# One-token gated decode on one core: the last half row of wo in 125 and 3 partitions, and three engine programs set to a block boundary

## The chip, the cores and the metric

The kernel runs on one core of one Trainium2 chip. The metric is the device time of one execution in microseconds (us), the median of several runs; lower is better.

## What is computed

One token passes through an attention block with a cached context and through a gated feed-forward block, and a sigmoid gate mixes the two results:

```python
g = sigmoid((x * gate_w).sum())                       # x: 512 values
q = x @ wq                                            # wq: 512 x 4096, 32 heads of 128
p = softmax((q . k_cache) * 128 ** -0.5)              # 8 kv heads x 32768 x 128, 4 query heads on each
a = (p . v_cache).reshape(4096) @ wo                  # v_cache like k_cache; wo: 4096 x 512
b = (silu(x @ w1) * (x @ w3)) @ w2                    # w1, w3: 512 x 1792; w2: 1792 x 512
out = g * a + (1 - g) * b                             # 512 values, all float32
```

Every weight and every cache entry is used once, so the work is mostly the transfer of the two caches (134 MB each) and the weights into the core's memory (SBUF).

## The kernel before, in words

Three SBUF regions, `ra`, `rb` and `rc`, hold 128 partitions x 16384 floats (64 KiB per partition, 8 MiB in all) each. Every large transfer is issued by SyncE (SP), in program order, on one hardware queue. A transfer with 128 partitions of contiguous rows moves one row into each partition.

The order of SP's transfers is written out by hand. First come wq into `rc` and w1, w3 into `rb` (line 36), issued ahead of a barrier of all engines (line 40), then the first half of head 0's keys into `ra` (L133). The loop of lines 138 to 148 issues, for each key/value head, two halves of keys (`ra`, `rb`) and two halves of values (`rc`), each behind a wait that says the region is free again: `c_k` counts the score products that PE has finished, `c_v` the value products. The last head's value halves go into `ra` and `rb` (L151, L153). Then come wo into `rc` as two halves of 128 x 8192 (L157, semaphores `l_wo[0]` and `l_wo[1]`), and, behind a wait on `c_v`, w2 into `ra` in five pieces (L163: 7, 4 and 2 of the 14 blocks of 512 columns; L166: the last block in two halves of 256 columns).

VectorE (DVE) turns the keys block by block (L368) in a hardware loop over the heads and does the maxima and the normalisation. TensorE (PE) runs a hardware loop over the heads as well: score products (L298), value products of the head before (L312), small transposes (L322). ScalarE (ACT) copies scores out of PSUM (L406), takes the exponentials (L412) and copies each head's output (L409); its program is unrolled over the eight heads. GpSimd (POOL) lays out the query windows, four copies for each head (L285), also unrolled.

The end of the kernel is PE's: with the heads' outputs in `oq`, 32 products of `oq` with the 32 blocks of 512 columns of wo (L444, the first 16 behind `l_wo[0]`, the others behind `l_wo[1]`), seven with w2's first piece (L451), and then w2's remaining blocks in quarters of 128 columns (L423), each piece behind its own semaphore. Two copies by DVE and ACT (L485) gather the result, ACT sends it out (L489), and SP waits for that transfer.

```python
wod = wo.rearrange("(p k) e -> p (k e)", k=32)
sp.wait_ge(c_v.sem, 2 * HKV - 2)
for i in range(2):
    sp.dma_start(rc[:, i * half:(i + 1) * half], wod[:, i * half:(i + 1) * half]).then_inc(l_wo[i], 16)
```

The functions that the change touches follow, with the profile's line numbers.

## Time and profile before

| what | value |
|---|---|
| median of 3 runs | 691.75 us (691.72 to 691.81) |
| the profiled execution's own time | 691.74 us |
| span of that execution, first to last instruction | 690.4 us |
| PE busy, share of the span | 349.7 us, 51% |
| DVE busy | 306.9 us, 44% |
| ACT busy | 41.6 us, 6% |
| POOL busy | 7.0 us, 1% |
| read from HBM | 296.23 MB, 429 GB/s over the span |

Busy times say how long an engine had an instruction in work. The core has 16 DMA engines; the shares given for them are means over the 16. The queue q1 carries SP's transfers, q10 ACT's; q8 and q14 carry instructions, which the engines' sequencers fetch in blocks while the program runs. A DMA view of a stretch books a packet by the time at which it starts.

### The profile page before, as it was taken

The numbers are of one execution on the slowest core, as the hardware profiler recorded it, in microseconds if no ns is written. First come the engines' busy times: TensorE is split into PE (matmuls) and PEld (weight loads), VectorE is DVE, ScalarE is ACT, GpSimd is POOL, SyncE is SP. The second block draws the span as 40 slices with busy tenths as digits, with TensorE's granted clock in tenths as the row PEclk, the third lists the DMA queues.
The fourth block names the chain that finished last, engine by engine and source line by source line (L and its number), as shares of the span: only waits on it lengthen the run. The fifth ranks groups of instructions, "written<-read, shape, count | busy, mean of one in ns | idle before, by whom it ended". The sixth has DMA issues, their size and how long they took to land. (4 is left out here: it accounts for less than half of the span.)

```text
span 690.4 us, 6719 instructions
## 1 busy us (share of the span) xinstructions
PE 349.7 (51%) x2946; PEld 112.6 (16%) x2946; DVE 306.9 (44%) x194; ACT 41.6 (6%) x111; POOL 7.0 (1%) x41
## 2 busy tenths in 40 slices
PE   1721645757065721757066721766075712766567
PEld 1200103103011120203021220203021210203122
DVE  1015862991725447091825447091815446191000
ACT  0110011002000010002000010002000010002000
POOL 0000000000000000000000000000000000000000
PEclk9985675988578965889567965988578965878679
DMA  9999999999999999999999999999999999999997
GB/s 414 393 469 426 425 426 427 444 448 429 426 425 440 425 437 452 429 429 425 437 429 429 456 433 429 425 433 433 425 444 444 430 429 425 437 429 429 452 411 320
DMA packets 6079, 296.36 MB, mean 429 GB/s; under 512 B 691, under 2 KB 947, under 8 KB 1078
## 3 DMA queue, kind: packets, MB, share of 16 engines
q1 hardware_dynamic: 6048, 296.23, 99.3%
q8 instruction: 6, 0.10, 0.1%
q14 instruction: 3, 0.02, 0.0%
q10 hardware_dynamic: 22, 0.01, 0.0%
HBM read 296.23 MB, written 0.00 MB: 429 GB/s over the span
## 5 line engine op out<-in xcount | busy, mean ns | idle before, releaser
L368 DVE STREAM_TRANSPOSE rb<-rb 128x2048 f32<-128x2048 f32 x64 | 141.8, 2275 | 130.7 <-DVEq L127 130.7
L312 PE MATMUL psum<-rc,prob 128*32 128x512 f32 x896 | 114.9, 671 | 140.5 <-PEq L127 140.5
L368 DVE STREAM_TRANSPOSE ra<-ra 128x2048 f32<-128x2048 f32 x64 | 141.3, 2274 | 58.3 <-DVEq L127 58.3
L298 PE MATMUL psum<-rb,winbuf 128*32 128x512 f32 x512 | 88.8, 771 | 84.9 <-PEq L127 84.9
L298 PE MATMUL psum<-ra,winbuf 128*32 128x512 f32 x512 | 60.9, 614 | 26.7 <-PEq L127 21.2
L312 PEld LDWEIGHTS psum<-rc,prob 128*32 128x32 f32 x896 | 34.2, 122 | 216.0 <-issue 216.0
L392 DVE TENSOR_REDUCE mx<-psum 128x4 f32<-128x1024 f32 x8 | 9.8, 1225 | 86.9 <-DVEq L127 86.9
L298 PEld LDWEIGHTS psum<-rb,winbuf 128*32 128x32 f32 x512 | 13.0, 120 | 159.1 <-issue 159.1
L406 ACT COPY sbuf<-psum 128x512 f32<-128x512 f32 x16 | 9.9, 616 | 471.1 <-PE psum L298 471.1
L298 PEld LDWEIGHTS psum<-ra,winbuf 128*32 128x32 f32 x512 | 16.8, 112 | 69.4 <-issue 69.4
L412 ACT ACTIVATE prob<-psum,nm 128x256 f32<-128x256 f32 x32 | 18.8, 693 | 47.0 <-DVE nm L400 47.0
L322 PE MATMUL psum<-ident,sbuf 128*64 128x64 f32 x512 | 18.1, 234 | 5.0 <-PEq L127 5.0
L322 PEld LDWEIGHTS psum<-ident,sbuf 128*64 128x64 f32 x512 | 17.0, 148 | 12.5 <-issue 12.5
L373 DVE SCALAR_TENSOR_TENSOR otall<-psum,gate,recip 128x4 f32 (+1 forms) x8 | 1.7, 214 | 33.3 <-DVEq L127 33.3
L345 PE MATMUL psum<-sums,ones 128*128 128x4 f32 x16 | 4.5, 350 | 22.8 <-PEq L127 22.8
L312 PE MATMUL psum<-rb,prob 128*32 128x512 f32 x64 | 8.8, 714 | 9.4 <-DMA rb<-in_A_v_cache_dram 9.4
L312 PE MATMUL psum<-ra,prob 128*32 128x512 f32 x64 | 9.9, 790 | 3.5 <-DMA ra<-in_A_v_cache_dram 3.5
L285 POOL COPY winbuf<-winraw 32x16 f32<-32x16 f32 x32 | 6.1, 190 | 535.7 <-PE psum L298 501.5
L444 PE MATMUL psum<-rc,oq 128*32 128x512 f32 x64 | 9.0, 712 | 3.9 <-DMA rc<-in_A_wo_dram 3.5
L229 PE MATMUL psum<-rc,xp 128*32 128x512 f32 x64 | 8.4, 687 | 4.7 <-DMA rc<-in_A_wq_dram 4.7
L256 PE MATMUL psum<-rb,xp 128*32 128x448 f32 x64 | 7.8, 637 | 5.4 <-DMA rb<-in_B_w_dram 5.3
L214 PE MATMUL psum<-ones,ob 1*128 1x1 f32 x8 | 2.0, 370 | 15.1 <-DMA prob<-in_gate_w_dram 15.1
(62 smaller groups left out, 86.4 us busy)
## 6 DMA issues: line engine op xcount, KB each, us to landing
rc<-in_A_wo_dram SPq DMA_DIRECT2D x2, 4096.0 KB, 45.8
rb<-in_B_w_dram SPq DMA_DIRECT2D x2, 3584.0 KB, 34.1
ra<-in_B_w_dram SPq DMA_DIRECT2D x1, 1792.0 KB, 33.0
ra<-in_B_w_dram SPq DMA_DIRECT2D x1, 1024.0 KB, 35.2
ra<-in_B_w_dram SPq DMA_DIRECT2D x1, 512.0 KB, 35.9
ra<-in_B_w_dram SPq DMA_DIRECT2D x2, 128.0 KB, 35.7
rc<-in_A_v_cache_dram SPq DMA_DIRECT2D x14, 31.1
ra<-in_A_k_cache_dram SPq DMA_DIRECT2D x8, 41.5
```

Source lines behind the costliest of these rows:

```text
L229: m = pe.matmul(pq[b][32 * j:32 * j + 32, :], xp[:, c, :], rc[:, o:o + REP * DH], start=(c == 0), stop=(c == NC - 1),)
L256: i = pe.matmul(ps[32 * j:32 * j + 32, 0:FJ], xp[:, c, :], rb[:, o:o + FJ], start=(c == 0), stop=(c == NC - 1))
L285: pool.tensor_copy(winbuf[32 * r:32 * r + 32, 16:144].rearrange("p (c k) -> p c k", k=32)[:, :, 4 * r:4 * r + REP], winraw[32 * r:32 * r + ...
L298: i = pe.matmul(s_ps[m][32 * g:32 * g + 32, :], winbuf[:, w:w + 32], region.rearrange("p (n c i) -> p c n i", c=4, i=32)[:, c, n:n + 16], ...
L312: i = pe.matmul(o_ps[32 * t:32 * t + 32, :], prob[:, w:w + 32], region[:, n * DH:(n + 4) * DH], start=(r == 0 and g == 0 and f == 0), stop ...
L322: i = pe.matmul(pf[64 * s:64 * s + 64, 64 * a:64 * a + 64], sbuf[:, a].rearrange("p i m -> p (i m)"), ident.rearrange("p (gf r s q) -> p s ...
L345: pe.matmul(mc[:, 0:REP], ones, sums, start=True, stop=True).then_inc(t_n, 1)
L368: dve.transpose(part[:, c], part[:, c]).then_inc(t_tr, 1)
L392: dve.tensor_reduce(mx, pf.rearrange("p (a q) -> p q a", q=REP), axis=AX.X, op=ALU.max).then_inc(t_mx, 1)
L406: act.copy(sbuf[:, :, :, m], s_ps[m].rearrange("p (n i) -> p n i", i=32)).then_inc(t_ev, 1)
L412: act.activation(prob[:, 0:1024].rearrange("p (a n q) -> p n a q", a=16, q=REP)[:, :, :, q], pf.rearrange("p (n a q) -> p n a q", n=16, q= ...
L444: pe.matmul(acc[32 * t:32 * t + 32, :], oq[:, k:k + 32], rc[:, k * D:(k + 1) * D], start=(k < 4), stop=False, skip_group_check=True,)
```

## The change

The diff has two parts.

In the first, an alignment directive is put on the programs of ACT, DVE and POOL, ahead of wq's load and of the barrier. It names 128 slots: where the loader places the program, the instruction that follows stands at a multiple of 128 instruction slots, and the slots skipped are branched over (`max_nops=0`). PE's and SP's programs get none.

In the second, the transfer of wo's second half loses its last 256 columns (half of the last block of 512), so that it moves 128 x 7936 instead of 128 x 8192. Those 256 columns come in two further transfers on the same queue behind it, of partitions 0 to 124 and of partitions 125 to 127. Both count on a new semaphore, `l_wx`, and PE waits for it ahead of the last of the 32 products with wo (k = 31).

```diff
+SHARE = 125
...
     nc = tc.nc
+    for engine in (nc.scalar, nc.vector, nc.gpsimd):
+        engine.addr_align(128, offset=0, max_nops=0)
     rb, rc = (nc.alloc_sbuf_tensor(n, [P, 16384], F32).ap() for n in ("rb", "rc"))
...
+    l_wx = token("l_wx")
...
     for i in range(2):
-        sp.dma_start(rc[:, i * half:(i + 1) * half], wod[:, i * half:(i + 1) * half]).then_inc(l_wo[i], 16)
+        e = slice(i * half, (i + 1) * half - i * D // 2)
+        sp.dma_start(rc[:, e], wod[:, e]).then_inc(l_wo[i], 16)
+    for p in (slice(0, SHARE), slice(SHARE, P)):
+        sp.dma_start(rc[p, W - D // 2:W], wod[p, W - D // 2:W]).then_inc(l_wx, 16)
...
             if k % 16 == 0:
                 pe.wait_ge(l_wo[k // 16], 16)
+            if k == 31:
+                pe.wait_ge(l_wx, 32)
```

SP's program from the last value half to the end, before (line, operation, region and source, partitions x elements):

```order
L153 DMA rb<-in_A_v_cache_dram 128x16384
L157 DMA rc<-in_A_wo_dram 128x8192 x2
L163 DMA ra<-in_B_w_dram 128x3584
L163 DMA ra<-in_B_w_dram 128x2048
L163 DMA ra<-in_B_w_dram 128x1024
L166 DMA ra<-in_B_w_dram 128x256 x2
```

and with the change, whose lines from 161 to 173 are those of wo and w2:

```order
L157 DMA rb<-in_A_v_cache_dram 128x16384
L162 DMA rc<-in_A_wo_dram 128x8192
L162 DMA rc<-in_A_wo_dram 128x7936
L164 DMA rc<-in_A_wo_dram 125x256
L164 DMA rc<-in_A_wo_dram 3x256
L170 DMA ra<-in_B_w_dram 128x3584
L170 DMA ra<-in_B_w_dram 128x2048
L170 DMA ra<-in_B_w_dram 128x1024
L173 DMA ra<-in_B_w_dram 128x256 x2
```

Two transfers more stand between wo's second half and w2; nothing else of SP moved.

The beginning of ACT's program, before:

```order
L519 UNCONDITIONAL_BRANCH
L40 UNCONDITIONAL_BRANCH
L169 DMA ob<-in_A_x_dram 1x512
L170 DMA prob<-in_gate_w_dram 1x8x64
L176 DMA out_dram<-sbuf 1x512
```

and with the change, where the directive is the row of line 32:

```order
L528 UNCONDITIONAL_BRANCH
L32 ISA
L43 UNCONDITIONAL_BRANCH
L176 DMA ob<-in_A_x_dram 1x512
L177 DMA prob<-in_gate_w_dram 1x8x64
L183 DMA out_dram<-sbuf 1x512
```

DVE and POOL get the same row at the same place.

## Rows read from the trace of the kernel before

**Rows 1.** The page: span, DMA busy tenths in 40 slices, queues (packets, MB, share).
```profile
span 690.4 us, 6719 instructions
...
DMA  9999999999999999999999999999999999999997
...
q1 hardware_dynamic: 6048, 296.23, 99.3%
q8 instruction: 6, 0.10, 0.1%
q14 instruction: 3, 0.02, 0.0%
q10 hardware_dynamic: 22, 0.01, 0.0%
```

**Rows 2.** Chain that ended last, in order of time: start us, us, what.
```profile
672.50 3.64 PE psum L444 x32
676.14 3.49 another core or an unknown queue
...
679.67 5.34 PE psum L444 x32
685.01 1.71 PE psum L451 x14
686.72 1.91 PE psum L423 x59
```

**Rows 3.** Line L157, the transfers of wo: ns min/median/max, issue times, then landing.
```profile
L157 SPq DMA_DIRECT2D rc<-in_A_wo_dram x2: 327/380/433, 628.8 to 629.1; - x2
...
DMA to landing us min/median/max: 41.2/45.8/50.5
```

**Rows 4.** Line L166, the last two transfers of w2.
```profile
L166 SPq DMA_DIRECT2D ra<-in_B_w_dram x2: 432/432/432, 652.2 to 652.7; - x2
...
DMA to landing us min/median/max: 35.6/35.7/35.8
```

**Rows 5.** Windows of the end: engines' busy us (x), PEclk, DMA share, GB/s.
```profile
680.00:685.00 5.00, 5.00 (x36) 1.39 (x32) 0.00 (x0) 0.00 (x0) 0.00 (x0) 0.66 0.98 411
...
686.60:687.00 0.40, 0.40 (x22) 0.40 (x23) 0.00 (x0) 0.22 (x1) 0.00 (x0) 1.00 0.45 172
687.00:687.30 0.30, 0.30 (x20) 0.30 (x13) 0.00 (x0) 0.30 (x1) 0.00 (x0) 1.00 0.35 123
687.30:687.60 0.30, 0.30 (x16) 0.16 (x12) 0.00 (x0) 0.06 (x1) 0.00 (x0) 1.00 0.34 120
687.60:688.00 0.40, 0.40 (x18) 0.31 (x20) 0.00 (x0) 0.00 (x0) 0.00 (x0) 1.00 0.13 44
```

**Rows 6.** DMA view by queue, stretch 60 to 680 us.
```profile
q8 instruction: 5, 0.08, 0.0%
```

**Rows 7.** DMA view, stretch 101 to 104 us (one of those five).
```profile
q8 instruction: 1, 0.02, 1.9%
```

**Rows 8.** DMA view, stretch 174 to 176 us.
```profile
q14 instruction: 1, 0.01, 1.0%
```

**Rows 9.** DMA view, stretch 545 to 551 us.
```profile
q14 instruction: 1, 0.01, 0.3%
```

**Rows 10.** DMA view, stretch 638 to 641 us.
```profile
q14 instruction: 1, 0.01, 0.7%
```

**Rows 11.** Timelines of ACT, POOL and DVE: what each ended shortly ahead of a q14 packet.
```profile
172.10 0.22 ACT L412 ACTIVATION_READ_ACCUMULATOR prob<-psum,nm 128x1 f32 x1
...
544.68 0.94 POOL L285 COPY winbuf<-winraw 32x16 f32<-32x16 f32 x4 [77.23 <-PE psum L298]
...
637.59 0.18 DVE L379 RECIPROCAL recip<-psum 128x4 f32<-128x4 f32 x1 [3.25 <-DVEq L127]
```

**Rows 12.** Timeline of the beginning: PE's first large products.
```profile
22.74 8.43 PE L229 MATMUL psum<-rc,xp 128*32 128x512 f32 x64 [4.70 <-DMA rc<-in_A_wq_dram]
```

**Rows 13.** DMA view, stretch 687 to 689 us (packets of 1 KiB, most of them).
```profile
q1 hardware_dynamic: 97, 0.09, 12.9%
```

## The prediction

> **What bounds the kernel now.** Read the page first. The DMA engines are busy at nine tenths or more in every slice but the last, and q1, SP's queue, takes 99.3% of their time for 296.23 MB, while no other engine is busy for much more than half the span [rows 1]. So the kernel lasts as long as its bytes need, and only three things can be saved: the start, the end, and unevenness between the 16 DMA engines. From these rows a packet's price follows: 0.993 x 16 x 690.4 us / 296.23 MB is 37.0 ns for 1000 bytes, 0.303 us for 8 KiB on one DMA engine.

> Second, the chain that ended last: it ends in PE's work on wo and w2, and holds a wait of 3.49 us from 676.14 us [rows 2]. Its end fits the landing of wo's second half: issued at 629.1 us, landed 50.5 us later, at 679.6 us; PE goes on at 679.67 us [rows 2, 3]. The very last link is also a landing: w2's last piece, issued at 652.7 us, lands 35.6 us later, at 688.3 us [rows 4], and the span ends 2.1 us after it. In between PE follows the landings closely.

> Third, the windows of the end, where the reader is to see how the DMA engines run dry: their share is 0.45, then 0.35 and 0.34, then 0.13 [rows 5]. Times 16 that is 7.2 engines busy on average from 686.6 to 687.0 us and 5.5 up to 687.6 us; the 0.13 over 0.4 us is 0.8 us of engine time, 0.17 us for each of five engines, so these end at about 687.8 us. Hence some nine engines are through by about 686.7 us, and **five end about 1.0 us later than the first ones do**. A transfer has landed only when its slowest engine is through, so the five set both landings.

> Fourth, what makes five late: five blocks of instructions on q8 between 60 and 680 us [rows 6]; the one shown took 1.9% of 16 x 3 us, 0.91 us of one DMA engine [rows 7]. PE's program is by far the longest, so I take them for its own; five late engines and five blocks of about 1 us, one to each, fit. The page's three q14 packets are smaller: 0.32 us (1.0% of 16 x 2), 0.3 us and 0.34 us [rows 8 to 10]. Each follows a step of another program: ACT's last exponential of a head at 172.10 us, POOL's last copies of all at 544.68 us, DVE's first instruction behind its loop at 637.59 us [rows 11]. I read them as fetches at the crossing of a block boundary, one for each of the three engines that the change aligns.

> **The change part by part.** *The alignment.* Programs that begin at a boundary cross one at their beginning, so the three fetches should move there. Removed: 0.3 us on three DMA engines that are not the latest (a lag of 0.3 us against 1.0 us), so nothing at the end; what hides it is the lag of the five. If the fetches come at the start and fall behind wq's packets, the three engines keep 0.3 us, again nothing, unless one is an engine that is late later: then +0.3 us. The branch over the padding can stall three programs ahead of the first barrier. No row shows such a stall; the cover is 4.70 us, the time that PE sits ready for wq [rows 12], and behind it all of SP's first transfers are queued without any wait. I take 0, and keep 0 to +0.3 us.

> *The 8 KiB taken off all 16 engines.* wo's second half shrinks from 32 to 31 KiB for each partition, 8 KiB on each engine: it lands 0.30 us earlier, and so does everything of w2 on an engine that gets no other rows.

> *The 125 and 3 rows.* How many engines take them? q1's 6048 packets are 42 transfers x 144: 16 engines with eight rows and one semaphore packet each. q10's 22 packets are four transfers of 1, 8, 1 and 1 rows, each row with one semaphore packet of its own: 1, 8, 1 and 1 engines [rows 1]. Rows are always shared out evenly, so I take five engines with 25 rows each, and three engines with one each. [...] A 1 KiB packet costs 43 ns, from 12.9% of 16 x 2 us over 97 packets; if the semaphore packets among them (one in nine) cost nothing, 48 ns; by bytes alone 38 ns [rows 1, 13]. I take 43, the row's own mean. A loaded engine then gets up to 26 x 43 ns = 1.12 us (0.99 to 1.25) and saves 0.30: it ends **0.82 us later** (0.69 to 0.95).

> *Where this lands.* If the five loaded engines are among the nine that are through by 686.7 us, they now end at about 687.5 us, and the five late ones, relieved, at 687.8 - 0.3 = 687.5 us. Both ends meet: the last landing comes 0.30 us earlier, or less where a loaded engine was not among the very first. The wait for wo's second half gets shorter by the same 0.30 us, so PE keeps its distance.

> *Around it.* Two more issues on SP, 0.43 us each [rows 3], come long before its next transfers: w2's last two follow only at 652.2 us, 23 us after wo [rows 3, 4]. PE's new wait stands before the last product with wo, 5.34 us behind the first of the second half [rows 2]; the loaded engines bring their rows 1.1 us behind wo's second half, so it costs nothing; without that cover, w2's products would queue behind it. The sum is **-0.30 us**: 691.74 us of the profiled execution becomes 691.44; the median shown is 691.75 us, so I say 691.45 us.

> [...]

> **The rivals.** *A, the forecast:* loaded and late engines are disjoint, -0.10 to -0.45 us, 691.3 to 691.65 us. *C, nothing moves:* a fetch at the start falls on a late engine (+0.3), or a loaded engine with a q14 fetch becomes the last; the -0.30 is eaten: 691.65 to 691.9 us. *B, the other side:* at least one late engine is among the loaded five; it gets 0.82 us more, PE's tail moves with it, 692.55 us (692.4 to 692.7). It decides from one common engine on. By pure chance five and five of 16 would nearly always meet, which speaks for B. [...] *E, one engine for 125 rows* (1 divides too): 125 x 43 ns = 5.4 us on it, some 696 us. *F, the change does not do what it says:* the loader's blocks are not 128 slots and the fetches stay; then the second part alone decides, again -0.30 us, inside A.

> **How the numbers follow.** A (with F) 0.66, C 0.16, B 0.12, D 0.03, E 0.01; 0.02 is left for a larger gain, which would need PE's q8 blocks to move too. 0.2% is 1.4 us, about what a measurement of this kernel can tell from no change. A, B and C all lie within it: levelling 16 engines of which five lag by 1.0 us can give at most 11/16 of that, 0.7 us, and B costs 0.8 us. So same 0.94, slower 0.04 (D, E), faster 0.02. A and C hold 0.82 of the chance and reach from 691.3 to 691.9 us; with the bounds of the packet price and the start, 691.1 to 692.0 us.

> **What would show it.** q1 has 42 x 144 + 130 + 6 = 6184 packets (five and three engines; 126 in place of 130 for one engine). No q14 packet lies between 10 and 680 us. L444 resumes at about 679.4 us; the share from 686.6 to 687.4 us is higher and falls off sooner. w2's last piece lands at about 688.0 us, for B at 689.2. The forecast is wrong if that landing is later than 688.3 us, or if PE is late behind it.

## The result, and the profile after

The changed kernel takes **692.73 us** (median of 22 runs, 692.46 to 693.09), the kernel before 691.78 us beside it (22 runs, 691.6 to 692.08): a ratio of 1.0014, interval 1.0007 to 1.002. The sign is sure, +0.95 us, and it is within the 0.2% that the prediction gave most of its chance to; but the predicted time was 691.45 us, and 692.73 lies outside the range of 691.1 to 692.0 us. One run with 25 rows of 5 KiB below (699.38 us, at a granted clock of 0.55 against some 0.76 in the others) and one of the kernel before beside it (696.09 us, at 0.61) stand apart, and move the ratios there, but not the medians.

The page of the changed kernel, as [rows 1]:

```profile
span 691.0 us, 6724 instructions
...
DMA  9999999999999999999999999999999999999997
...
q1 hardware_dynamic: 6184, 296.23, 99.4%
q8 instruction: 6, 0.10, 0.1%
q14 instruction: 4, 0.03, 0.0%
```

The bytes are the same, and 6184 packets on q1 are what five engines with 25 rows and three with one give. The kernel is still bound by its transfers; the span is 0.6 us longer in the profiled execution (itself the shortest of the 22, 692.46 us, against 691.74 us for the profiled one of before). Its chain that ended last, against [rows 2]:

```profile
650.52 36.56 DMA ra<-in_B_w_dram
687.07 0.04 issue
687.12 2.13 PE psum L430 x60
```

and the line of w2's last two transfers, against [rows 4]:

```profile
L173 SPq DMA_DIRECT2D ra<-in_B_w_dram x2: 8345/9011/9677, 651.5 to 661.2; - x2
...
DMA to landing us min/median/max: 27.8/32.5/37.2
```

The last piece, issued at 661.2 us, lands 27.8 us later, at 689.0 us; before it was 688.3 us. The span ends 2.0 us behind it, before 2.1 us. So PE is not late behind the landing, and what has to be explained is why **w2's last piece lands 0.7 us later** in this execution, where 0.30 us earlier was forecast: past the 688.3 us beyond which the prediction called itself wrong. (The issue itself takes 9 us here in place of 0.43: more on that at the end.)

Where the time went is in the windows. First the three microseconds up to the landing of wo's second half, and then the end, as [rows 5]:

```profile
677.00:680.00 3.00, 2.98 (x20) 0.67 (x12) 0.00 (x0) 0.00 (x0) 0.00 (x0) 0.64 0.97 312
686.60:687.00 0.40, 0.00 (x0) 0.00 (x0) 0.00 (x0) 0.40 (x1) 0.00 (x0) 1.00 0.73 287
687.00:687.30 0.30, 0.18 (x8) 0.18 (x12) 0.00 (x0) 0.19 (x1) 0.00 (x0) 1.00 0.65 249
687.30:687.60 0.30, 0.30 (x20) 0.30 (x15) 0.00 (x0) 0.00 (x0) 0.00 (x0) 1.00 0.65 239
687.60:688.00 0.40, 0.40 (x24) 0.40 (x17) 0.00 (x0) 0.00 (x0) 0.00 (x0) 1.00 0.50 174
688.00:688.50 0.50, 0.50 (x20) 0.28 (x16) 0.00 (x0) 0.00 (x0) 0.00 (x0) 1.00 0.36 98
```

The same three microseconds of the kernel before:

```profile
677.00:680.00 3.00, 0.33 (x4) 0.16 (x8) 0.00 (x0) 0.00 (x0) 0.00 (x0) 1.00 0.88 373
```

Read the last two columns together. Before, a share of 0.88 moves 373 GB/s: 0.88 x 16 / 373 is 37.7 ns of a DMA engine for 1000 bytes. After, a *higher* share of 0.97 moves only 312 GB/s: **49.7 ns for 1000 bytes**. The engines are not idle, each packet takes longer (by the packets' records w2's pieces of 14 KiB that start from 677.8 to 680 us take 691 ns at the median, 536 ns before), and this is the stretch in which the 125 rows are on their way. At 37.7 ns a share of 0.97 would have moved 0.97 x 16 / 37.7, 411 GB/s; over 3 us the 99 GB/s that are missing are 297 KB, 18.6 KB on each of 16 engines, and at 37.7 ns that is **0.70 us for every engine**. Neither the sum nor a rival had such a term. At the end ten engines are still busy from 687.3 to 687.6 us (0.65 x 16), where it was 5.5.

The two DMA views for the alignment, 0 to 8 us and 640 to 643 us, against [rows 8 to 10]:

```profile
q14 instruction: 3, 0.02, 1.4%
...
q14 instruction: 1, 0.01, 0.6%
```

Three fetches lie at the start now and one is left, at 641 us, one more in all than before. Those at the start meet the first loads: three take 1.4% of 16 x 8 us, 1.8 us together, 0.6 us each on the mean (0.78, 0.66 and 0.31 us by the packets' records) where one took 0.3 us in mid-run.

### The profile page after: what moved, and what is told of

The parts are those of the page before. It is cut to its first block, busy times and chain, and to the rows that moved or that the text cites. A ratio compares the mean times of both kernels' runs of the same rounds, so it can differ in the third digit from the quotient of the medians.

```text
span 691.0 us, 6724 instructions
## 1 busy us (share of the span) xinstructions
PE 364.5 (53%) x2946; PEld 113.5 (16%) x2946; DVE 306.9 (44%) x194; ACT 41.7 (6%) x111; POOL 7.0 (1%) x41
## 3 DMA queue, kind: packets, MB, share of 16 engines
q1 hardware_dynamic: 6184, 296.23, 99.4%
HBM read 296.23 MB, written 0.00 MB: 429 GB/s over the span
## 5 line engine op out<-in xcount | busy, mean ns | idle before, releaser
L319 PE MATMUL psum<-rc,prob 128*32 128x512 f32 x896 | 116.7, 679 | 136.8 <-PEq L131 136.8
L305 PE MATMUL psum<-rb,winbuf 128*32 128x512 f32 x512 | 98.9, 854 | 78.6 <-PEq L131 78.6
L305 PE MATMUL psum<-ra,winbuf 128*32 128x512 f32 x512 | 62.4, 628 | 25.2 <-PEq L131 20.3
## 6 DMA issues: line engine op xcount, KB each, us to landing
rc<-in_A_wo_dram SPq DMA_DIRECT2D x1, 4096.0 KB, 39.7
```

What stands on the lines that cost most here:

```text
L305: i = pe.matmul(s_ps[m][32 * g:32 * g + 32, :], winbuf[:, w:w + 32], region.rearrange("p (n c i) -> p c n i", c=4, i=32)[:, c, n:n + 16], ...
L319: i = pe.matmul(o_ps[32 * t:32 * t + 32, :], prob[:, w:w + 32], region[:, n * DH:(n + 4) * DH], start=(r == 0 and g == 0 and f == 0), stop ...
```

## The experiments

The first four take the change apart. Medians are set against the kernel before beside them (691.82 to 691.85 us).

**The split alone.** The diff of the change without the lines of the alignment.

> The split of wo's last half row into 125 and 3 partitions, without the alignment. Theory 1 (two causes: the 1 KiB rows on few DMA engines slow all engines for about 2 us and eat the 0.30 us that was to be saved; the alignment puts two instruction fetches on wq's first packets of two engines, which are then loaded with the 125 rows and end last): about no change, 691.6 to 692.0 us, DMA rate in the microsecond after wo's end well under 300 GB/s as in the changed kernel. Theory 2 (rival B of the prediction: an engine that is late from a PE fetch is among the five loaded ones): all of the loss and more, 692.4 to 692.8 us. Theory 3 (the alignment delays the whole kernel by the 0.6 us of its later barrier): 691.45 us.

Measured: 692.56 us (692.29 to 693.0), ratio 1.001, interval 1.0001 to 1.0019. The window of 677 to 680 us:

```profile
677.00:680.00 3.00, 3.00 (x24) 0.72 (x17) 0.00 (x0) 0.00 (x0) 0.00 (x0) 0.64 0.99 322
```

0.99 x 16 / 322 is 49.2 ns for 1000 bytes. The split by itself brings the slow stretch, and +0.72 us of the +0.95. The time is the one that the expectation gave to theory 2, but the windows show the slow stretch of theory 1, which costs more than that theory allowed.

**The alignment alone.**

```diff
+    for engine in (nc.scalar, nc.vector, nc.gpsimd):
+        engine.addr_align(128, offset=0, max_nops=0)
```

> The alignment alone, wo in two halves as before. Theory 1: two engines get a lag of about 0.7 us at the start, less than the 1.0 us of the five engines with PE's fetches, so the end does not move: 691.7 to 691.95 us; q14 packets at about 1.7 us. Theory 2: 691.75 us. Theory 3 (the later barrier moves all by 0.6 us): 692.3 us.

Measured: 691.86 us (691.64 to 692.08), ratio 1.0001, interval 0.9992 to 1.001.

```profile
677.00:680.00 3.00, 0.26 (x4) 0.16 (x8) 0.00 (x0) 0.00 (x0) 0.00 (x0) 1.00 0.88 373
```

This is the row of before. The alignment is worth nothing here, as the sum had it, though three fetches went to the start, where the prediction's second case put them; one stayed, at 639 us.

**The same piece in one transfer of 128 rows.**

```diff
-    for p in (slice(0, SHARE), slice(SHARE, P)):
-        sp.dma_start(rc[p, W - D // 2:W], wod[p, W - D // 2:W]).then_inc(l_wx, 16)
+    sp.dma_start(rc[:, W - D // 2:W], wod[:, W - D // 2:W]).then_inc(l_wx, 16)
...
-                pe.wait_ge(l_wx, 32)
+                pe.wait_ge(l_wx, 16)
```

> The same half row as one transfer of its own with all 128 partitions (eight 1 KiB rows on each of the 16 engines), no alignment. If the slowness comes from few engines writing far partitions: no slow stretch, 691.75 to 691.85 us. If it comes from reading 1 KiB rows at wo's pitch of 64 KiB (memory side): slow stretch stays, all engines lose 0.3 us or more, 692.0 to 692.3 us.

Measured: 691.92 us (691.73 to 692.12), ratio 1.0002, interval 0.9993 to 1.0011.

```profile
677.00:680.00 3.00, 3.00 (x24) 0.86 (x20) 0.00 (x0) 0.00 (x0) 0.00 (x0) 0.65 0.95 388
```

0.95 x 16 / 388 is 39.2 ns. A third transfer, a new wait and 128 pieces of 1 KiB are harmless. PE's clock and busy time are those of the split alone, so neither explains its slow stretch. What is left is that few engines carry the rows, or that it matters into which partitions they write.

**Other memory rows.** The 125 and 3 rows are read from w2, whose rows lie 28 KiB apart and not 64 KiB as wo's do; the last half row of wo is left out of the computation.

```diff
+    w2f = w2.rearrange("(p k) e -> p (k e)", k=FR)
     for p in (slice(0, SHARE), slice(SHARE, P)):
-        sp.dma_start(rc[p, W - D // 2:W], wod[p, W - D // 2:W]).then_inc(l_wx, 16)
+        sp.dma_start(rc[p, W - D // 2:W], w2f[p, FR * D - D // 2:FR * D]).then_inc(l_wx, 16)
```

> Split in 125 and 3 without the alignment, but the two transfers read rows of w2 (28 KiB apart) instead of wo's (64 KiB apart), so that the last half row of wo is left out of the computation and replaced by a piece of w2. If the memory side with its pitch of 64 KiB makes the slow stretch: it goes, 691.4 to 691.55 us. If few engines make it: as the split alone.

Measured: 692.53 us (692.33 to 692.88), ratio 1.0011, interval 1.0002 to 1.002.

```profile
677.00:680.00 3.00, 2.73 (x20) 0.60 (x16) 0.00 (x0) 0.00 (x0) 0.00 (x0) 0.72 0.95 307
```

0.95 x 16 / 307 is 49.5 ns: the stretch stays. The distance of 64 KiB between the rows in memory is not the cause.

The next seven leave the transfers of the kernel before as they are and put an *extra* one ahead of w2, from wo's rows into a part of ra that nobody reads. From one to the next its form changes, and with four, eight or ten rows its bytes too. (One wait for it is added at the very end of SP.)

**Five rows spaced by 8, 25 pieces of 1 KiB each.**

```diff
+    sp.dma_start(ra[0:40:8, 8192:14692].rearrange("p (a c) -> p a c", c=260)[:, :, 0:256], wod[0:40:8, 0:12800].rearrange("p (a c) -> p a c", c=512)[:, :, 0:256]).then_inc(l_wx, 16)
...
+    sp.wait_ge(l_wx, 16)
```

> [...] Theory S (long strings of 1 KiB pieces on few engines slow all): 200 to 300 GB/s for a microsecond, 692.5 us or more. Theory B (one of the five is late from a PE fetch): no slow stretch but 692.9 us.

Measured: 693.17 us (692.95 to 693.56), ratio 1.0016, interval 1.0006 to 1.0027.

```profile
677.00:680.00 3.00, 0.00 (x0) 0.00 (x0) 0.00 (x0) 0.00 (x0) 0.00 (x0) 1.00 0.91 266
```

54.7 ns, slower than with the 125 rows. By itself this run fits theory S, with 246 to 287 GB/s in slices of 1 us and 693.17 us.

**125 rows of 1 KiB.**

```diff
+    sp.dma_start(ra[0:125, 8192:8448], wod[0:125, W - 256:W]).then_inc(l_wx, 16)
```

> [...] Theory B: no slow stretch, 692.9 us.

Measured: 692.79 us (692.5 to 693.28), ratio 1.0011, interval 1.0 to 1.0021.

```profile
677.00:680.00 3.00, 0.40 (x4) 0.00 (x0) 0.00 (x0) 0.00 (x0) 0.00 (x0) 1.00 0.89 285
```

50.0 ns: what the split does, without the split.

**25 rows of 5 KiB.**

```diff
+    sp.dma_start(ra[0:25, 8192:9472], wod[0:25, 0:1280]).then_inc(l_wx, 16)
```

> The same extra 125 KiB as 25 rows of 5 KiB into partitions 0 to 24 (five engines, five rows each). [...] Theory B: 692.9 us without a slow stretch.

Measured: 692.86 us (692.64 to 699.38), ratio 1.0019, interval 1.0001 to 1.0037 (by the medians 1.0015).

```profile
677.00:680.00 3.00, 0.00 (x0) 0.00 (x0) 0.00 (x0) 0.00 (x0) 0.00 (x0) 1.00 0.89 299
```

47.6 ns. Five pieces on an engine in place of 25, the same bytes, and still slow: small pieces are not the cause, against theory S.

**Ten rows spaced by 8.** As with five, `0:80:8`.

> [...] If the engines that are late from PE's fetches lie among the second five: 692.9 us. [...]

Measured: 694.76 us (694.24 to 695.29), ratio 1.0038, interval 1.0027 to 1.0048.

```profile
677.00:680.00 3.00, 2.40 (x16) 0.45 (x8) 0.00 (x0) 0.00 (x0) 0.00 (x0) 0.76 0.86 201
```

68.5 ns. With ten engines and twice the rows all are held up more than with five. That is odd if too few engines were the trouble, and suggests that it matters where they write.

The last four runs change the partitions of the extra rows, and in the split the number of engines.

**Five rows spaced by 4.** `0:20:4` in place of `0:40:8`, all else as in the run with five rows spaced by 8.

> The kernel before with an extra transfer ahead of w2: 25 pieces of 1 KiB on each of partitions 0, 4, 8, 12 and 16, five DMA engines again. [...] Theory F (any transfer that few engines carry holds all of them up): 215 to 300 GB/s between 677 and 681 us and about 693.2 us, as with the rows spaced by 8.

Measured: 692.33 us (692.03 to 692.61), ratio 1.0007, interval 0.9998 to 1.0016.

```profile
677.00:680.00 3.00, 0.24 (x4) 0.16 (x8) 0.00 (x0) 0.00 (x0) 0.00 (x0) 1.00 0.87 357
```

0.87 x 16 / 357 is 39.0 ns, against 54.7 ns with as many engines, pieces and bytes spaced by 8: **the slow stretch is gone, and the partitions were changed.** With them the rows of wo that are read changed too, from 512 to 256 KiB apart; that this matters isn't excluded by this pair alone, but rows 28 and 64 KiB apart were slow above. The slices of 1 us go as low as 292 GB/s because engines were idle there (share 0.74, so 40.5 ns), not slow; the ratio of the two columns is what tells. Theory F, that any transfer of few engines holds up all of them, falls. The +0.51 us (the interval just reaches 1) is that of a loaded engine that becomes the last. Which one, the packets' records tell: on one engine a packet starts 3 to 4 ns before the one ahead of it ends, so that each engine can be followed through the trace, though no view does it. It is a loaded engine that also had the q14 fetch of 639 us; 25 pieces 43 ns apart are 1.1 us, and it lands at 688.98 us where the last landing of before was 688.34 us.

**Eight rows spaced by 4.** `0:32:4`.

> The same with eight rows, partitions 0 to 28 by fours, eight DMA engines, each with 25 more pieces of 1 KiB (1.0 us at 38 ns a piece). [...] F: the slow stretch of 215 to 300 GB/s is there, 693 us or more; if F holds only for five engines and fewer, none.

Measured: 692.7 us (692.14 to 692.92), ratio 1.0012, interval 1.0003 to 1.0021.

```profile
677.00:680.00 3.00, 0.81 (x12) 0.16 (x8) 0.00 (x0) 0.00 (x0) 0.00 (x0) 1.00 0.89 359
```

39.7 ns: again no slowing. w2's last piece lands 27.5 us after 661.9 us, at 689.4 us, 1.0 us later than before: nearly the whole price of 25 pieces, as it must be where a late engine is among the loaded. With five engines it landed at 689.0 us (27.4 us after 661.6). Followed by packets, two of the eight loaded engines are ones with a q8 block, and they end last; with five loaded there is none, in the one execution of each that was profiled.

**Four neighbouring rows.** `0:4` in place of `0:40:8`: partitions 0 to 3.

> [...] F: as with five rows, 50 to 60 ns a piece, some 1.5 us, about 693 us. [...]

Measured: 695.02 us (694.76 to 695.45), ratio 1.0048, interval 1.0035 to 1.0062. Slices of 1 us:

```profile
678.00:679.00 1.00, 0.61 (x8) 0.00 (x0) 0.00 (x0) 0.00 (x0) 0.00 (x0) 1.00 1.27 260
679.00:680.00 1.00, 0.00 (x0) 0.00 (x0) 0.00 (x0) 0.00 (x0) 0.00 (x0) 1.00 1.18 133
680.00:681.00 1.00, 0.00 (x0) 0.00 (x0) 0.00 (x0) 0.00 (x0) 0.00 (x0) 1.00 0.94 115
681.00:682.00 1.00, 0.00 (x0) 0.00 (x0) 0.00 (x0) 0.00 (x0) 0.00 (x0) 1.00 0.67 130
```

The fewest bytes of all extra transfers, 100 KiB, cost the most, +3.2 us. In the packets' own records (no view groups them) the engine that begins first goes through its 25 pieces at 46 to 54 ns each; the other three begin at 46 ns and come to 189 to 222 ns. From 679.8 to 680.6 us each of the three starts a piece every 176 ns, 17 GB/s for all three, where one engine alone starts one every 43 ns, 24 GB/s: **into these four partitions three engines together bring no more than one engine alone does.** The others slow down with them, to 131 ns for 1000 bytes on the mean of 16 from 680 to 681 us (0.94 x 16 / 115), though twelve have no extra row. By what path it spreads to the twelve, these rows don't show.

**The split with 120 and 8 rows.** `SHARE = 120`, without the alignment.

> [...] F (few engines): no slow stretch, 691.85 us. [...]

Measured: 692.45 us (692.16 to 692.76), ratio 1.001, interval 1.0001 to 1.0019.

```profile
677.00:680.00 3.00, 3.00 (x21) 0.72 (x17) 0.00 (x0) 0.00 (x0) 0.00 (x0) 0.59 0.97 313
```

49.6 ns, with fifteen engines of eight rows each (its 6199 packets are 42 x 144, 120 + 15 and 8 + 8). No engine has more than nine rows, and the kernel is still 0.63 us slower. So the missing bytes are nearly the whole loss: by the same reckoning as above, 0.97 x 16 / 37.7 is 411, less 313, times 3 us, 0.69 us for every engine.

## Why the prediction was wrong

**What bounds the kernel** held: transfers bind it, a landing sets the end, and PE follows 2.0 us behind the last one.

**The alignment** came out at its predicted nothing (+0.02 us alone, within the interval), but not by its mechanism. Not all of the fetches went to the beginning: one on q14 stayed at 641 us, against the marker that none lies between 10 and 680 us. And a fetch at the start is dearer, 0.6 us on the mean where 0.3 us was taken. Whether it adds to the split, 692.73 against 692.56 us with overlapping ranges, is open. In the change the two engines that end last, at 688.95 and 688.99 us, are loaded ones that by the packets' records had a fetch at the start; but in the split without the alignment the last landing, at 689.18 us, is a loaded engine's too, so this does not tell them apart.

**The number of engines** was right, five and three, by the 6184 packets. That both transfers meet on the same engines, from which the 26th piece in 26 x 43 ns comes, was my estimate, and no row or run shown here tells it; the changed kernel's trace shows 128 pieces of 1 KiB, of 46 ns each at first and of 67 ns at the median from 677.8 to 680 us.

**The step that failed first** is the one that prices the split: *the 8 KiB taken off all 16 engines* was to bring "everything of w2 on an engine that gets no other rows" 0.30 us forward, and *the 125 and 3 rows* were charged to the loaded engines alone, at 43 ns a piece, the price of w2's last pieces, which come in transfers of 128 rows. Both assume that an engine's packet costs the same whatever else is being written. The runs show that it does not: with a transfer of 120 or 125 rows beside them the packets go from 37.7 to about 50 ns for 1000 bytes on the mean of 16 engines while it lasts (49.2 to 50.0 in the five kernels with such a transfer; 37.7 to 39.7 in the kernel before, the alignment alone, the 128 rows and the five and eight rows spaced by 4). That is some 0.70 us on all 16 engines. For an unloaded engine -0.30 becomes +0.40, for a loaded one +0.82 becomes about +1.5. By the trace's landings of w2's last piece on each engine, the first engine of all lands at 687.00 us in place of 686.64, the late ones at 688.4 to 688.8 us in place of 688.1 to 688.3, and the loaded ones up to 688.99.

**A second step failed:** that the five loaded engines are among the nine that are through by 686.7 us. Followed by packets, the kernel before has its five q8 blocks on the five engines that land last, 688.09 to 688.34 us, as the prediction took it, and its three q14 fetches on the next three, 687.27 to 687.63 us. The five loaded engines (traced in the split from w2's rows, in the extra transfers of 125 rows, of 25 rows of 5 KiB and of five rows spaced by 4) are none of the late ones, but three of them are these q14 engines. By the prediction's own +0.82 us the last of them lands at 687.63 + 0.82 = 688.45 us, 0.1 us behind the last landing of before, so that the -0.30 us was gone even without a slow stretch. An estimate from these two steps, 0.1 + 0.70 us, is near the +0.72 us of the split alone.

I took the piece to be slower on its own engines alone, and did not ask what else becomes slower. A term "what a transfer of another form does to the packets beside it", without a row of before to price it, ought to have stood in the range with a bound above zero.

**Rival B** gave 692.55 us, close to the result, but for another reason. A late engine among the loaded five isn't needed: 120 and 8 rows lose 0.63 us with no engine that has more than nine rows, and by the packets no late engine is among the five. That loaded and late engines are disjoint, on which rival A's 0.66 rests, was my estimate, which no row of before shows; the traces named above bear it out. **Rival C's** loaded engine with a q14 fetch is what ends last in the traces named above; its 691.65 to 691.9 us lacked the 0.70 us that all pay. **D**, a lower granted clock of PE up to the end, and **E** did not occur: PE's clock is lower from 677 to 680 us in the split (0.64; 1.00 before), but as low in the harmless transfer of 128 rows (0.65), and 1.00 from 686.6 us on in the changed kernel; 6184 packets exclude one engine.

**The levelling itself** did not win in either form measured: 125 and 3 rows and 120 and 8 rows both bring the slow stretch (49.2 to 49.7 ns), and its 0.70 us on every engine is more than the 0.30 us taken off. A split without the slow stretch that relieves the late engines wasn't tried, and whether there is one isn't shown. No version here beats the kernel before.

## What to carry to other kernels

## What the runs showed that I had not expected

- A transfer of 100 KiB into four neighbouring partitions took all 16 DMA engines down to 115 GB/s and cost 3.2 us; the same kind of transfer, 125 KiB into five partitions spaced by 4, cost 0.5 us.
- SP's last issues of w2 took 17 to 18.5 us in place of 0.9, in every kernel with an extra transfer or a split that puts 25 pieces on an engine, and not where it was eight or five (128 rows, 120 and 8 rows, 25 rows of 5 KiB). The timeline of SP after and before:

```profile
651.46 18.07 SPq L173 DMA_DIRECT2D ra<-in_B_w_dram x2
```

```profile
652.24 0.91 SPq L166 DMA_DIRECT2D ra<-in_B_w_dram x2
```

I take it to have cost nothing, since these transfers are queued 27 us or more ahead of their landing; 25 rows of 5 KiB are slow without it. Whether it costs anything in a kernel whose SP has something else to do, no run shows.
- An instruction fetch on q14 at the start, beside wq's first packets, took 0.6 us of a DMA engine on the mean of three; in mid-run one took 0.31 to 0.33 us.
